# Seven products of halves for 256 channels of gate and up, from chunk 4 on, with partial sums kept in PSUM

## The chip, the cores and the metric

The kernel runs on one core of one Trainium2 chip, in float32 inputs and outputs. The metric is the time of one execution on the device, in microseconds; the kernel before takes 1945.81 us, the median of 3 runs (1944.42 to 1949.61). The engines: PE multiplies matrices (PEld is its loading of weights), DVE, ACT and POOL work element by element, and SP here issues the DMAs. Each engine takes its instructions strictly in the order in which the program wrote them.

## The reference

One block of a network over x of 8192 rows (tokens) and 448 channels, in two halves:

```python
mod = (_silu(c) @ w_mod).reshape(c.shape[0], 6, 1, -1)
sa, ca, ga, sb, cb, gb = (mod[:, 0], mod[:, 1], mod[:, 2], mod[:, 3], mod[:, 4], mod[:, 5])
h = _layernorm(x) * (1 + ca) + sa
x = x + ga * spectral(h)           # rfft, two complex block layers, shrinkage, irfft
h = _layernorm(x) * (1 + cb) + sb
x = x + gb * ((_gelu(h @ w_gate) * (h @ w_up)) @ w_down)    # 448 -> 1792 -> 448
```

The change touches the last two lines.

## The kernel before

Up to 390 us of the profile the spectral part runs; its last inverse transform is done later, chunk by chunk. What follows is the feed-forward part: 32 chunks (`nch`) of 256 rows, each as two blocks b of 128. Float32 accuracy comes from splitting: every operand is a high and a low f16 part, and a product is three matmuls (high x high, high x low, low x high).

**Gate and up** (`gate_up`, L1124). Each chunk has 14 blocks k of 128 features; k = 2t and 2t + 1 are a pair t with q = 0, 1. The feature block is the weight side (128x128), the rows are the moving side (256 columns), and gate and up (pr = 0, 1) lie in one PSUM bank. The 448 channels are three tiles of 128 and a fourth, composed tile that holds the last 64 channels' high and low parts. So a block takes 20 full matmuls in the order of `seq` (L1132), and one half-row matmul for each pr, over 64 channels, which two pairs share in a batch of eight (L1140), two at a time on the upper and lower half of the array. Then `gate_up_out` (L1148): gelu on ACT (L1151), gate times up on DVE (L1156) into x8 tiles and, once both q are there, four additions and subtractions on POOL (the "sums", L1162 to L1165), which prepare the down product. `quantize` (L1167) makes the f16 pair: ACT the high part (L1173), DVE the low part (L1174). It is called one pair later.

**Down** (`down`, L1186) has already seven products of halves in place of eight: 147 matmuls of 224 columns (L1181 to L1183), after k = 2 of the following chunk. Its order on PE is p1 and the 1,1 product (b1, b2), then p4, u2, u4, p7, p3. Product banks rotate over two of tag "pd" (and one of "pc" for b2), so that the product for u2 needs the bank that ACT's copy of p1 (L1208) frees. POOL finishes the output (L1220, L1195, L1196) and SP stores it (L1228).

**Preparing a chunk.** `hooks` (L1233) say behind which block k of a chunk each step for a later chunk stands: loads at k = 0; splitting of v and g (ACT, and POOL at L124) at 3; `inverse` (six f32 matmuls on PE) at 6; `residual` at 7; statistics, square root and normalisation at 8 to 12 (DVE); at 13 `pack_hi` (ACT) and `pack_lo` (POOL, L1077 to L1079). `transposes_dma` (L1081) turns 16 tiles of 128x128 by DMA on SP's queue, one chunk ahead, at k = 0. All of it is under manual schedule: the order of the program is the order on each engine, and nothing is reordered. In the profiled execution chunk 2 begins at 478.35 us, and its down product, that of chunk 1, at 485.55.

## Time and profile before

| | |
|---|---|
| median of 3 runs | 1945.81 us |
| profiled execution: time, span | 1943.83 us, 1942.0 us |
| mean granted clock of PE | 0.993 |
| time of chunk 2 (478.35 to 526.35 us) | 48.00 us |
| DVE, ACT, POOL busy in it | 25.24, 15.46, 31.14 us |

How to read the lines below: a line of the timeline is start, length, engine, source line and operation, what is written and read, how many instructions, and in brackets the idle time ahead of it with what ended it. In a group, the two numbers behind the bar are busy time in all and the mean length of one instruction in nanoseconds. [...] "issue" means that nothing in the profile shows a wait.

### The profile page before, as it was taken

What the parts mean: (1) busy time and instruction counts of PE and PEld (TensorE: products, weight loads), DVE (VectorE), ACT (ScalarE), POOL (GpSimd) and SP (SyncE); (2) the same over time, 40 slices, a digit from 0 to 9 for tenths busy, and PEclk for the clock granted to TensorE, in tenths of its full rate; (3) what the DMA queues carried; (4) which work ended last, traced back from release to release, by engine and by line L of the source; (5) the groups of instructions that cost most, each with busy time, mean ns of one, the idle gap of its engine ahead of it and who ended that gap; (6) DMA issues with size and microseconds to landing.
All of it is one profiled execution on the core that took longest, in us unless ns stands there. A gap on an engine that the chain in (4) does not pass through costs nothing.

```text
span 1942.0 us, 43274 instructions
## 1 busy us (share of the span) xinstructions
PE 1899.8 (98%) x17606; PEld 1690.5 (87%) x17606; DVE 1130.9 (58%) x2340; ACT 779.2 (40%) x1325; POOL 1209.8 (62%) x1492
## 2 busy tenths in 40 slices
PE   7799999899999999999999999999999999999998
PEld 3599999688888888888888888888888888888898
DVE  7687889677555555555555555555555555555533
ACT  5677788553333333333333333333333333333322
POOL 3366689355666666666666666666666666666644
PEclk9899999899999999999999999999999999999999
DMA  9888768431111111111111111111111111111000
GB/s 388 289 275 253 223 192 246 136 97 54 43 44 44 44 43 43 44 43 43 44 44 43 44 43 44 44 43 43 44 43 44 43 44 44 43 43 44 21 16 20
DMA packets 144398, 164.39 MB, mean 85 GB/s; under 512 B 85062, under 2 KB 117062, under 8 KB 143814
## 3 DMA queue, kind: packets, MB, share of 16 engines
q1 hardware_dynamic: 144198, 161.62, 27.6%
q8 instruction: 138, 2.26, 0.5%
q14 instruction: 62, 0.51, 0.1%
HBM read 98.29 MB, written 47.25 MB: 75 GB/s over the span
## 4 chain that ended last, share of the span: by engine, by line
PE 78%; DVE 1%; POOL 1%; DMA 1%; ACT 0%; issue 0%; SPq 0%; POOLq 0%; ACTq 0%
PE pgu L1115 53%; PE pdn L1183 8%; PE pdn L1182 8%; PE pdn L1181 8%; PE pi L1015 1%; PE pi L1013 1%; PE pi L1014 1%; DMA dr<-wdd 0%; DVE ac L1174 0%; DVE n L1065 0%; POOL x L1163 0%; DVE n L1064 0%; DMA vd<-us 0%; POOL x L1162 0%; DMA v<-vd 0%
## 5 line engine op out<-in xcount | busy, mean ns | idle before, releaser
L1115 PE MATMUL pgu<-nt,wh 128*128 128x256 f16 x6272 | 832.8, 273 | 0.2 <-DVE nt L1106 0.2
L1115 PEld LDWEIGHTS <-wh 128*128 128x128 f16 x6272 | 602.0, 98 | 97.3 <-issue 30.3
L1151 ACT ACTIVATE gel<-pgu,dg 128x256 f32<-128x256 f32 x448 | 200.0, 473 | 779.8 <-PE pgu L1115 744.8
L1115 PE MATMUL pgu<-nt,wl 128*128 128x256 f16 (+1 forms) x3584 | 500.9, 272 | 0.7 <-DVE x L1156 0.7
L1183 PE MATMUL pdn<-wd,ac 128*128 128x224 f16 x1568 | 406.1, 259 | 1.1 <-DVE ac L1174 1.1
L1181 PE MATMUL pdn<-wd,ac 128*128 128x224 f16 x1568 | 406.1, 259 | 0.0
L1182 PE MATMUL pdn<-wd,ac 128*128 128x224 f16 x1568 | 406.1, 259 | 0.0
L1162 POOL TENSOR_TENSOR x<-x 128x128 f32<-128x128 f32 x223 | 240.5, 1078 | 241.1 <-DVE x L1156 233.3
L1174 DVE SCALAR_TENSOR_TENSOR ac<-x,sa_act,ac 128x896 f16<-128x896 f32 (+1 forms) x225 | 308.3, 1370 | 86.5 <-ACT ac L1173 86.5
L1115 PEld LDWEIGHTS <-wl 128*128 128x128 f16 (+1 forms) x3584 | 297.6, 97 | 57.6 <-issue 24.6
L1156 DVE TENSOR_TENSOR x<-pgu,gel 128x256 f32<-128x256 f32 x448 | 179.0, 417 | 271.4 <-ACT gel L1151 270.7
L1173 ACT ACTIVATE ac<-x,sa_act 128x896 f16<-128x896 f32 (+1 forms) x225 | 233.0, 1035 | 57.3 <-POOL x L1165 55.2
L1220 POOL TENSOR_TENSOR o<-u,p 128x224 f32<-128x224 f32 x32 | 21.4, 667 | 300.8 <-DVE u L1219 300.8
L1163 POOL TENSOR_TENSOR x<-x 128x128 f32<-128x128 f32 x223 | 159.3, 714 | 17.5
L1183 PEld LDWEIGHTS <-ac 128*128 128x128 f16 x1568 | 153.4, 98 | 1.6 <-DVE ac L1174 1.6
L1181 PEld LDWEIGHTS <-ac 128*128 128x128 f16 x1568 | 153.4, 98 | 0.8 <-ACT ac L1173 0.3
L1182 PEld LDWEIGHTS <-ac 128*128 128x128 f16 x1568 | 153.4, 98 | 0.4
L1164 POOL TENSOR_TENSOR x<-x 128x128 f32<-128x128 f32 x223 | 113.4, 509 | 0.0
L1165 POOL TENSOR_TENSOR x<-x 128x128 f32<-128x128 f32 x223 | 110.5, 496 | 0.0
L561 POOL TENSOR_TENSOR yl<-y,yh 128x448 fp32r<-128x448 f32 x63 | 75.5, 1213 | 40.3 <-ACT yh L556 36.4
L1195 POOL TENSOR_TENSOR o<-o,gb_r 128x448 f32<-128x448 f32 (+1 forms) x64 | 71.9, 1123 | 11.2 <-DVE o L1209 5.6
L1214 DVE TENSOR_TENSOR u<-pdn,p 128x224 f32<-128x224 f32 x32 | 12.5, 392 | 110.9 <-PE pdn L1183 110.9
(268 smaller groups left out, 2870.3 us busy)
## 6 DMA issues: line engine op xcount, KB each, us to landing
raw<-in_gu SPq DMA_DIRECT2D x28, 512.0 KB, 5.4
vd<-us SPq DMA_DIRECT2D x64, 224.0 KB, 3.3
xx<-in_x SPq DMA_DIRECT2D x32, 448.0 KB, 3.2
v<-vd SPq DMA_DIRECT2D x64, 224.0 KB, 2.8
out<-x SPq DMA_DIRECT2D x31, 448.0 KB, 2.7
tr<-td SPq DMA_DIRECT2D x22, 448.0 KB, 6.9
nt<-pk SPq DMA_TRANSPOSE x488, 2.3
tb<-in_x SPq DMA_DIRECT2D x8, 896.0 KB, 17.9
```

The source lines that it names most:

```text
L1115: T.matmul(pgu[i, t, q][:, pr * H : (pr + 1) * H], w[rows, tw, f0 : f0 + 128], nts[i][rows, tn, :], start=start, stop=stop, skip_group_che ...
L1151: S.activation(gl, ps[:, :H], AF.Gelu_apprx_tanh, scale=dg)
L1156: V.tensor_tensor(dst, ps[:, H : 2 * H].rearrange("p (b c) -> p b c", b=2), gl.rearrange("p (b c) -> p b c", b=2), ALU.mult)
L1162: e.tensor_tensor(s1, a21, a22, ALU.add)
L1163: e.tensor_tensor(s2, s1, a11, ALU.subtract)
L1164: e.tensor_tensor(s3, a11, a21, ALU.subtract)
L1165: e.tensor_tensor(s4, a12, s2, ALU.subtract)
L1173: S.activation(ac[:, 0, k], x[:, k], AF.Copy, scale=sc)
L1174: V.scalar_tensor_tensor(ac[:, 1, k], x[:, k], sc, ac[:, 0, k], op0=ALU.mult, op1=ALU.subtract)
L1181: T.matmul(ps, ac[:, 0, ka], wds[t][:, 0, kb], start=t == 0, stop=False)
L1182: T.matmul(ps, ac[:, 0, ka], wds[t][:, 1, kb], start=False, stop=False)
L1183: T.matmul(ps, ac[:, 1, ka], wds[t][:, 0, kb], start=False, stop=t == NP - 1)
```

## The change

From chunk 4 on (`C0`), gate and up of the first two channel tiles are done as one 2x2 product of halves: channels 0 to 127 and 128 to 255 on the one side, row blocks b, feature blocks q = 0, 1. Seven products of 128 columns (Winograd's form) stand for eight. Each is again three matmuls for gate and three for up. The third and fourth channel tile stay as they were (`rest`, `rest_half`), with 256 columns.

The partial sums of the seven products stay in PSUM: a pair has two banks, E and D, from two rings of three. ACT copies one quarter of E to D, another to SBUF (`c5`) and one inside E, DVE adds twice with a result in PSUM, and PE goes on accumulating on what they wrote. A pair passes through three periods: `front1` and `front2`, then `mid`, then `back_e` and `back_d` with gelu, product and sums. quant_hi comes one period later, quant_lo two. One period works on three pairs.

```diff
+        def front1(a):
...
+            prod(a, e, 1, a_of(t, 0, 0), 0, True)
+            prod(a, e, 0, a_of(t, 1, 0), 4)
+            d = ds[a] = ring("D", n)
+            S.copy(quarter(d, 0), quarter(e, 1))
...
+            S.copy(c5, quarter(e, 0))
+        def front2(a):
+            prod(a, es[a], 1, s_of(a[1], 0), 5)
+            V.tensor_tensor(quarter(ds[a], 1), quarter(es[a], 1), c5s[a], ALU.add)
+        def mid(b):
+            e = es[b]
+            prod(b, e, 1, s_of(b[1], 2), 6)
+            S.copy(quarter(e, 0), quarter(e, 1))
+            V.tensor_tensor(quarter(e, 1), quarter(e, 1), c5s.pop(b), ALU.add)
+        def back_e(c):
+            e = es[c]
+            prod(c, e, 0, a_of(c[1], 1, 1), 7)
+            rest(c, 1, e)
+            rest_half(c)
+            out_gelu(*c, 1, e)
+        def back_d(c):
+            d = ds[c]
+            prod(c, d, 0, a_of(c[1], 0, 1), 2)
+            prod(c, d, 1, s_of(c[1], 1), 3)
+            rest(c, 0, d)
+            out_gelu(*c, 0, d)
+            out_mult(*c, 0, d)
+            out_sums(*c)
+        def period(n, hook):
+            a, b, c = (pair(n - j) for j in range(3))
+            if a:
+                front1(a)
+            if n == C0 * NP:
+                quantize(C0 - 1, NP - 1)
+            if pair(n - 4) and (n - 4) % NP != NP - 1:
+                quant_lo(*pair(n - 4))
+            if b:
+                mid(b)
+            hook(0)
+            if c:
+                back_e(c)
+            if a:
+                front2(a)
+            if c:
+                out_mult(*c, 1, es.pop(c))
+            if pair(n - 3):
+                quant_hi(*pair(n - 3))
+            if c:
+                back_d(c)
+                del ds[c]
+            hook(1)
```

The sums of weights (three for each t and pr) are made in chunk 2, one block behind each k; in chunk 3 one more sum overwrites a weight that is no longer needed as it was. Both load their raw weights again by DMA on SP's queue, into two buffers:

```diff
+        def make_s(t, pr):
+            r = raws_s.pop((t, pr)).rearrange("p i k c -> p (i k) c")
...
+            G.tensor_tensor(r[:, 3], r[:, 2], r[:, 3], ALU.add)
+            G.tensor_tensor(r[:, 2], r[:, 0], r[:, 2], ALU.subtract)
+            G.tensor_tensor(r[:, 0], r[:, 3], r[:, 0], ALU.subtract)
+            G.tensor_tensor(r[:, 1], r[:, 1], r[:, 0], ALU.subtract)
+            w_split(shs[t][:, 0, pr], shs[t][:, 1, pr], r[:, 0:3], pr)
+        for i in range(C0):
...
             for k in range(NFT):
                 gate_up(i, k)
...
                 if k == 2 and i > 0:
                     down(i - 1)
...
+                run_hooks(hooks, i, k)
+                t, pr = divmod(k, 2)
+                if i == C0 - 2:
+                    if k > 0:
+                        make_s(*divmod(k - 1, 2))
+                    load_s(t, pr, 0)
+                if i == C0 - 1:
+                    if k == 0:
+                        make_s(NP - 1, 1)
+                    elif k > 1:
+                        make_s1(*divmod(k - 2, 2))
+                    if k > 0:
+                        load_s(*divmod(k - 1, 2), 1)
```

`w_split` is one operation on ACT and one on DVE. The preparation of a chunk moves. From chunk 4 on `hooks2` holds, keyed by 2t + 0 (`hook(0)`) or 1:

```diff
+        hooks2 = {
+            2: [(2, split_g), (2, split_v)],
+            4: [(1, transposes_dma, 0, 16), (2, inverse, slice(0, D), "pd"), (2, residual)],
+            12: [(2, pack_hi)],
+            13: [(2, pack_lo)],
+        }
+        amid = {
+            "b1": [(stats2,), (rsqrt_part, 5)],
+            "b2": [(rsqrt_part, 9), (norm2, 0)],
+            "u2": [(norm2, 1)],
+            "u4": [(combos,)],
+        }
```

`amid` puts statistics and normalisation between the DVE steps of down, which now stands behind t = 2 of the next chunk, and whose b2 is also a "pd" bank. `combos` is four new subtractions of 128 columns on DVE, which make the sums of rows and channels. `pack_hi` and `pack_lo` take 1280 columns (768 in the subtraction before), and a chunk has 22 DMA transposes: 16 at t = 2, the other six behind down and its store. One normalised buffer now holds the low part of v too, and the scales of the rows and weights are made smaller by a power of two. At the end, behind the last period, quant_lo of the third-last pair, quant_hi and quant_lo of the second-last one and both of the last stand ahead of the last down.

## The prediction

> **What bounds the kernel now.** I read the page first: busy time by engine, and the chain that ended last.

> ```profile
> PE 1899.8 (98%) x17606; PEld 1690.5 (87%) x17606; DVE 1130.9 (58%) x2340; ACT 779.2 (40%) x1325; POOL 1209.8 (62%) x1492
> PE pgu L1115 53%; PE pdn L1183 8%; PE pdn L1182 8%; PE pdn L1181 8%; PE pi L1015 1%; PE pi L1013 1%; PE pi L1014 1%; DMA dr<-wdd 0%; DVE ac L1174 0%; DVE n L1065 0%; POOL x L1163 0%; DVE n L1064 0%; DMA vd<-us 0%; POOL x L1162 0%; DMA v<-vd 0%
> L1115 PE MATMUL pgu<-nt,wh 128*128 128x256 f16 x6272 | 832.8, 273 | 0.2 <-DVE nt L1106 0.2
> L1115 PEld LDWEIGHTS <-wh 128*128 128x128 f16 x6272 | 602.0, 98 | 97.3 <-issue 30.3
> ...
> L1156 DVE TENSOR_TENSOR x<-pgu,gel 128x256 f32<-128x256 f32 x448 | 179.0, 417 | 271.4 <-ACT gel L1151 270.7
> ```

> TensorE, nothing else: gate and up (L1115) are half of the chain and wait 0.2 us in all. So work taken from PE is time saved, as long as no other engine gets in PE's way. The windows of chunk 2 and of a later chunk give the others' load, and the timeline gives the cadence:

> ```profile
> core 0: us, PE busy (x) PEld busy (x) DVE busy (x) ACT busy (x) POOL busy (x), PEclk, DMA share, GB/s
> 478.35:526.35 48.00, 48.00 (x459) 42.97 (x456) 25.24 (x51) 15.46 (x25) 31.14 (x41) 1.00 0.22 64
> ...
> 1001.01 0.93 PE L1115 MATMUL pgu<-nt,wh 128*128 128x256 f16 x7
> 1002.10 0.93 PE L1115 MATMUL pgu<-nt,wh 128*128 128x256 f16 x7
> ```

> Seven plus three matmuls start in 1.09 us: 109 ns for 256 columns. POOL works 31 of 48 us; it is the fullest engine after PE, and its queue is in order.

> **PE: what the change saves.** Per pair of feature blocks, before: 40 matmuls of 256 columns (4.36 us) and half of a batch of eight half-row matmuls. After: 7 products x 2 (gate, up) x 3 = 42 matmuls of 128 columns, each with a weight load of its own, 16 of 256, and four half-row ones. The prices of the narrow and the half-row ones:

> ```profile
> 205.38 0.22 PE L410 MATMUL ps<-s,th 128*112 128x128 f16 x1
> ...
> 205.99 0.22 PE L412 MATMUL ps<-s,tl 128*112 128x128 f16 x1
> ```
> ```profile
> 1008.32 1.03 PE L1115 MATMUL pgu<-nt,wl 128*128 128x256 f16 x11
> 1009.29 0.94 PE L1115 MATMUL pgu<-nt,wh 128*128 128x256 f16 x7
> 1009.28 0.66 PEld L1115 LDWEIGHTS <-wh 128*128 128x128 f16 x7 [0.21 <-issue]
> ```

> The spectral stage already runs 128-column f16 matmuls that each load new weights: twelve starts from 205.38 to 205.99, 55.5 ns each. The batch of eight halves costs 1009.29 - 1008.32 less three full ones, 0.64 us, so 0.32 a pair. They go two at a time (0.109 us per two), and the remaining 0.20 us is the pause around the batch, which the change pays for every pair: 0.22 + 0.20 = 0.42. After: 42 x 0.0555 + 16 x 0.109 + 0.42 = 2.33 + 1.74 + 0.42 = 4.50 us; before: 4.68. **Saved: 0.185 us a pair, 36 us over 28 x 7 pairs.** The pause eats a third of what seven products instead of eight give.

> [...]

> **The build of the sums' weights (chunks 2 and 3).** Each k of chunk 2 loads two raw blocks, makes sums on POOL (four 128x128 operations), rounds on ACT and subtracts on DVE. The load sits on SP behind the 16 transposes of the next chunk, and POOL and ACT wait for it in order:

> ```profile
> 482.43 21.27 SPq L1085 DMA_TRANSPOSE nt<-pk  x16
> 510.37 0.46 SPq L917 DMA_DIRECT2D g<-cgm  x1
> g<-cgm SPq DMA_DIRECT2D x32, 128.0 KB, 2.9
> 478.35 0.82 PE L1115 MATMUL pgu<-nt,wh 128*128 128x256 f16 x6
> 485.55 0.26 PE L1181 MATMUL pdn<-wd,ac 128*128 128x224 f16 x1
> 489.49 0.35 ACT L1208 COPY p<-pdn 128x224 f32<-128x224 f32 x1 [3.26 <-PE pdn L1183]
> 491.79 0.35 ACT L1213 COPY p<-pdn 128x224 f32<-128x224 f32 x1 [1.95 <-PE pdn L1183]
> 1925.08 0.62 ACT L1173 ACTIVATE ac<-x,sa_act 128x384 f16<-128x384 f32 x1 [1.19 <-DVE x L1156]
> ```

> SP is free of the transposes at 503.7; the first load is two DMAs of 128 KB, each like that of g (0.46 us to issue, 2.9 to land), and is there at about 507.3. POOL's four sums (each 0.42 us, rows below) end at 509.0, ACT's 384-wide rounding at 509.6. The copy of p1 (L1208) stands behind it on ACT, and behind one gelu: 510.4 instead of 489.5. PE has the next product's bank only then; it was ready at 491.7. **Stall: 18.6 us.** Between the two copies PE ran 24 matmuls in 2.30 us, 96 ns each; down's 147 take 14.1. From 510.4 PE needs 84 of them (8.0 us), eleven blocks (24.0), three batches of halves (1.9) and about 1 for an inverse: to 545. POOL has, from 507.3 on, 13 blocks' four sums (21.5 us) and most of the chunk's own 31.1 us (some 25: five pairs' sums, the output's, the split, the residual): to 554, and between them it waits for ACT and DVE. PE is **10 us late** (0 to 18).

> In chunk 3 the transposes are 22 (29.2 us at that row's 1.33 each), starting 4.1 us into the chunk (482.43 - 478.35). The one-block load behind them lands at 36.6 us, ACT is held from the end of down until 37.3, and gelu and product free the banks at 38.4. PE wants them after three blocks (20 matmuls of 0.109 each, 6.5 us), 14.1 of down, three more blocks and a batch of halves (7.2): 27.8. **Stall: 10.6 us.** Together 39 us (20 to 55; below 0 is excluded, nothing is removed here).

> **The new steady state, 28 chunks.** Work that comes onto other engines in a 4.50 us period: ACT three copies of 128x256, DVE two additions whose result goes to PSUM. No row writes PSUM from ACT or DVE; the nearest are the 0.35 us copy above and DVE's L1156 at 0.42. I take 0.37 and 0.42. With two gelus and one quant_hi ACT then works 3.1 of 4.50 us, and DVE with two products and one quant_lo 2.8; at twice the price 4.2 and 3.7. PE's next use is a good microsecond away, so these cost nothing by themselves. What does cost is order:

> ```profile
> 1001.81 0.72 DVE L1156 TENSOR_TENSOR x<-pgu,gel 128x256 f32<-128x256 f32 x2
> 1002.45 1.14 DVE L1174 SCALAR_TENSOR_TENSOR ac<-x,sa_act,ac 128x896 f16<-128x896 f32 x1
> 1002.62 1.29 POOL L1162 TENSOR_TENSOR x<-x 128x128 f32<-128x128 f32 x1 [1.60 <-DVE x L1156]
> 1003.99 0.46 POOL L1163 TENSOR_TENSOR x<-x 128x128 f32<-128x128 f32 x1
> 1004.41 0.45 POOL L1164 TENSOR_TENSOR x<-x 128x128 f32<-128x128 f32 x1
> 1004.83 0.45 POOL L1165 TENSOR_TENSOR x<-x 128x128 f32<-128x128 f32 x1
> 1005.31 1.04 ACT L1173 ACTIVATE ac<-x,sa_act 128x896 f16<-128x896 f32 x1 [0.35 <-POOL x L1165]
> 1002.30 0.47 ACT L1151 ACTIVATE gel<-pgu,dg 128x256 f32<-128x256 f32 x1 [0.63 <-PE pgu L1115]
> ```
> ```profile
> 1014.66 0.43 POOL L1077 TENSOR_TENSOR pk<-n,pk 128x128 f16<-128x128 f32 x1
> 1015.03 0.30 POOL L1078 COPY pk<-pk 128x128 f16<-128x128 f16 x1
> 1015.28 1.65 POOL L1079 TENSOR_TENSOR pk<-n,pk 128x768 f16<-128x768 f32 x1
> 1015.81 2.06 DVE L1174 SCALAR_TENSOR_TENSOR ac<-x,sa_act,ac 128x896 f16<-128x896 f32 x1 [1.01 <-ACT ac L1173]
> 1016.88 1.31 POOL L1162 TENSOR_TENSOR x<-x 128x128 f32<-128x128 f32 x1
> 1036.81 0.73 POOL L124 TENSOR_TENSOR gl<-g,gh 128x256 fp32r<-128x256 f32 x1
> 1037.49 2.10 POOL L124 TENSOR_TENSOR vl<-v,vh 128x896 fp32r<-128x896 f32 x1
> ```

> The four sums take 2.75 us from the end of DVE's product (1002.53 to 5.28), since the first one runs against DVE's quant_lo (1.29 instead of 0.46); alone they take 1.65. Now follow one period: gelu 0.47, product 0.42, sums 2.75, quant_hi 1.04, two hand-overs of 0.03 (1005.28 to 1005.31), then the next gelu behind it on ACT: a loop of 4.74 us against PE's 4.50. It slips 0.24 us a period from t = 3 on, some 0.8 us by the next chunk's t = 0; down, with its 14 us of PE work, resets it.

> Then POOL's queue over the chunk border. The diff puts the split of g and v in t = 1 and the inverse that needs it in t = 2, one period apart; before, three blocks lay between. Ahead of the split on POOL are, from t = 0: sums (2.75, from the product's end at 1.1 us: 0.2 for PE's last result, gelu, product; 1.9 with the slip), pack_lo with 1280 instead of 768 columns (0.37 + 2 x 0.27 + 2.75 = 3.6), quant_lo's turn in it (0.83, as 1015.81 and 1016.88 show: one waits for the other), the next sums (1.65), then gl and vl (2.8). That is 11.6 us: vl is there at 12.7 to 13.5 us. PE wants it in the third matmul of the inverse: two periods (9.0), 18 narrow matmuls (1.0) and two of 448 columns (0.4) into the chunk, at 10.4. **Stall: 2.3 to 3.1 us, I take 2.7, in 26 chunks (inverse for chunks 6 to 31): 70 us.** With no clash at all it would be 0.4 (10 us).

> Other edits: statistics and normalisation moved into down run on DVE there with some 0.5 us to spare before PE wants a bank (0, at most 14 us in all). 22 transposes end some 3 us before they are used: 0; what is late next is pack_hi, on ACT. Filling the pipeline: 2 us; the end, where quant of the last pairs comes behind the last matmuls: 2 us.

> **Sum,** on the profiled execution: 1943.8 - 36 + 39 + 70 + 4 = 2021. It lies 2 us under the median of the runs, 1945.8, so I say 2022.

> **Rivals.** (1) *PE alone counts:* loads come early and POOL keeps up, as its 62% suggests. 1945.8 - 36 + 0 to 15 = 1910 to 1925. Against it: the queues are in order, and each of the waits follows from their order. 0.12. (2) *Only the build is paid:* POOL and DVE clash less than in the rows and the split is there in time: 1945.8 - 36 + 39 + 4 + up to 13 = 1953 to 1966. 0.15. (3) *Weight loads bound the narrow matmuls,* so that seven products are dearer than eight: it decides from 62 ns a matmul on (24 wide ones, 2.616 us, over 42). For it: a load's own row is 98 ns (PEld, L1115), and a narrow matmul gives it only 54 ns of streaming to hide under. At the full 98 ns PE takes 42 x 0.0425 = 1.78 us more in each of 196 pairs, 350 us, but POOL is then in time: 1945.8 - 36 + 39 + 4 + 350 = 2303, and less in proportion to what is hidden. Against it: the 55.5 ns. 0.03. [...] (4) *DVE is late in down as well,* 0.5 to 1 us in each of 28 chunks, on top of the forecast and its larger stalls: 2055 to 2090. 0.05. My forecast, build and POOL's queue together, 1975 to 2055: 0.65.

> **Numbers.** A measurement here tells 0.3% (6 us) from no change. Faster: rival 1 (0.12) and a part of rival 2 (0.03), where half of the build is hidden too; same 0.05, from rival 2 again; slower 0.80. The range of 1950 to 2055 leaves out rivals 1, 3 and 4, which hold 0.20.

> **What would show it.** Narrow products 55 to 56 ns apart; a pair at 4.50 us where PE does not wait; in chunk 2's down a hole of 18 us ahead of its fourth product, ended by ACT's copy of p1; in chunk 3 one of 10 us; once a chunk a hole of 2 to 3 us in the inverse, ended by POOL's vl. I am wrong if PE stays at 98% (rival 1), if the holes lie elsewhere, or if the products stand further apart than 62 ns.

## The result, and the profile after

The kernel after takes 2108.13 us (median of 4 runs, 2105.63 to 2112.41), the kernel before 1945.12 in the runs beside it: a ratio of 1.084 (1.081 to 1.086). The change makes the kernel slower by 163 us, where 77 were forecast. The profiled execution has a span of 2105.9 us. Its page, busy times, granted clock, the start of the chain and the groups that are new:

```profile
PE 1940.9 (92%) x21137; PEld 1706.1 (81%) x21137; DVE 1298.7 (62%) x2877; ACT 981.3 (47%) x1942; POOL 1252.8 (59%) x1591
PEclk9899999898888999999999999999999999999999
PE 36%; POOL 28%; ACT 7%; DVE 5%; issue 3%; SPq 2%; DMA 1%; POOLq 0%; ACTq 0%
L1280 PE MATMUL ring<-nt,wh 128*128 128x128 f16 x3136 | 332.8, 222 | 11.2 <-DVE x L1224 11.2
L1325 ACT COPY ring<-ring 128x256 f32<-128x256 f32 x196 | 70.0, 357 | 325.1 <-PE ring L1280 249.8
L1331 DVE TENSOR_TENSOR ring<-ring,rc 128x256 f32<-128x256 f32 x196 | 84.4, 430 | 125.2 <-PE ring L1280 125.0
```

PE is no longer on the chain for nearly all of the span: POOL, ACT and DVE have 40% of it. The copies and additions inside PSUM cost 357 and 430 ns, against the 0.37 and 0.42 us of the forecast. And the row PEclk, by fortieths of the span, is 8 four times in a row where the weights' sums are built (474 to 684 us); its two other dips are in the kernel before as well. The mean granted clock is 0.957, before 0.993. Next, from the timeline of PE in a later chunk, the groups at which a period starts and the inverse:

```profile
996.60 0.39 PE L1309 MATMUL ring<-nt,wl 64*128 64x256 f16 x4
...
1001.12 0.39 PE L1309 MATMUL ring<-nt,wl 64*128 64x256 f16 x4
1001.45 0.51 PE L1280 MATMUL ring<-nt,sh 128*128 128x128 f16 x6
1001.79 0.28 PE L1280 MATMUL ring<-nt,wh 128*128 128x128 f16 x2
...
1017.48 0.27 PE L1280 MATMUL ring<-nt,wh 128*128 128x128 f16 x2 [0.42 <-DVE x L1224]
1018.46 0.45 PE L1036 MATMUL pi<-vo,gh 128*128 128x448 f32 x1
1018.86 0.47 PE L1037 MATMUL pi<-vo,gl 128*128 128x448 f32 x1
1020.90 0.47 PE L1038 MATMUL pi<-vn,gh 128*128 128x448 f32 x1 [1.58 <-POOL vn L125]
...
1022.21 0.85 PE L1294 MATMUL ring<-nt,wh 128*128 128x256 f16 x3
...
1026.03 0.49 PE L1294 MATMUL ring<-nt,wh 128*128 128x256 f16 x3
```

Where nothing waits, a period is 1001.12 - 996.60 = 4.52 us (forecast 4.50), and six narrow products take 1001.79 - 1001.45 = 0.34 us, 57 ns each (from start to start; the row of a single one is 222 ns long, as L1280 above shows). So PE's own saving is there. The hole in the inverse is there too, ended by POOL's vl (the tile is named vn here). What no row of the forecast has is the line at 1022.21: three matmuls of 256 columns take 0.85 us, and 4 us later 0.49. The same stretch in windows of 3.41 us:

```profile
core 0: us, PE busy (x) PEld busy (x) DVE busy (x) ACT busy (x) POOL busy (x), PEclk, DMA share, GB/s
1015.26:1018.67 3.41, 2.99 (x44) 2.69 (x41) 2.17 (x4) 1.76 (x4) 3.33 (x6) 1.00 0.06 14
1018.67:1022.09 3.42, 1.84 (x11) 1.14 (x11) 2.51 (x4) 1.81 (x5) 3.42 (x3) 1.00 0.11 22
1022.09:1025.50 3.41, 3.41 (x26) 2.23 (x24) 1.14 (x4) 0.79 (x2) 3.33 (x6) 0.50 0.15 31
1025.50:1028.91 3.41, 3.41 (x41) 3.32 (x39) 2.01 (x4) 1.09 (x2) 0.95 (x2) 1.00 0.14 29
```

The start of the down product in each chunk, read from the trace, tells where the 163.9 us between the two spans (2105.9 and 1942.0) arise:

| stretch | before | after | difference | forecast |
|---|---|---|---|---|
| to down in chunk 2 | 485.5 | 485.0 | -0.5 | 0 |
| from there to down in chunk 4 (build and filling) | 96.5 | 187.7 | +91.2 | 39, and 2 for filling |
| from there 25 chunks on | 1205.6 | 1275.4 | +69.8 | 25 x (2.7 - 1.3) = 35 |
| from there to the last down | 135.2 | 131.7 | -3.5 | -3.9 |
| the last down | 14.4 | 21.3 | +6.9 | 2 |

The last row ends with the last matmul; what follows it takes some 4.8 us in both kernels. Of the 25 chunks in the third row, 21 hold one window at half clock and take 51.2 us; four hold none and take 49.7. Before, they took 48.0 and 48.5 in turn.

### The profile page after: what moved, and what is told of

The parts are those of the page before. It is cut to its first block, busy times and chain, and to the rows that moved or that the text cites. A ratio compares the mean times of both kernels' runs of the same rounds, so it can differ in the third digit from the quotient of the medians.

```text
span 2105.9 us, 51710 instructions
## 1 busy us (share of the span) xinstructions
PE 1940.9 (92%) x21137; PEld 1706.1 (81%) x21137; DVE 1298.7 (62%) x2877; ACT 981.3 (47%) x1942; POOL 1252.8 (59%) x1591
## 3 DMA queue, kind: packets, MB, share of 16 engines
q1 hardware_dynamic: 182502, 172.65, 27.8%
## 4 chain that ended last, share of the span: by engine, by line
PE 36%; POOL 28%; ACT 7%; DVE 5%; issue 3%; SPq 2%; DMA 1%; POOLq 0%; ACTq 0%
POOL x L1232 9%; PE pdn L1414 7%; PE pdn L1416 7%; PE pdn L1415 7%; PE ring L1280 6%; PE ring L1294 6%; ACT ac L1240 4%; POOL x L1233 4%; POOL pk L1126 3%; POOL x L1235 3%; DVE x L1224 3%; POOL vn L125 3%; ACT gel L1215 2%; SPq L1146 2%; POOL x L1234 2%
## 5 line engine op out<-in xcount | busy, mean ns | idle before, releaser
L1232 POOL TENSOR_TENSOR x<-x 128x128 f32<-128x128 f32 x223 | 275.9, 1237 | 328.5 <-DVE x L1224 320.2
L1414 PE MATMUL pdn<-wd,ac 128*128 128x224 f16 x1568 | 409.2, 261 | 23.9 <-ACT p L1445 18.1
L1294 PE MATMUL ring<-nt,wh 128*128 128x256 f16 x2352 | 379.4, 280 | 0.0
L1224 DVE TENSOR_TENSOR x<-ring,gel 128x256 f32<-128x256 f32 x392 | 164.6, 420 | 308.7 <-ACT gel L1215 308.7
L1280 PE MATMUL ring<-nt,wh 128*128 128x128 f16 x3136 | 332.8, 222 | 11.2 <-DVE x L1224 11.2
L1280 PE MATMUL ring<-nt,sh 128*128 128x128 f16 x3528 | 298.6, 221 | 13.8 <-ACT rc L1327 13.6
L1280 PE MATMUL ring<-nt,wl 128*128 128x128 f16 x1568 | 298.7, 222 | 0.0
L1215 ACT ACTIVATE gel<-ring,dg 128x256 f32<-128x256 f32 x392 | 183.7, 469 | 197.9 <-PE ring L1309 163.3
L1280 PEld LDWEIGHTS <-wh 128*128 128x128 f16 x3136 | 251.9, 99 | 27.2 <-issue 23.7
L1280 PEld LDWEIGHTS <-sh 128*128 128x128 f16 x3528 | 217.3, 99 | 63.7 <-issue 63.7
L1294 PEld LDWEIGHTS <-wh 128*128 128x128 f16 x2352 | 220.3, 101 | 22.0
L1294 PE MATMUL ring<-nt,wl 128*128 128x256 f16 x784 | 219.3, 280 | 0.0
```

Source lines behind the costliest of these rows:

```text
L1215: S.activation(gl, ps[:, :H], AF.Gelu_apprx_tanh, scale=dg)
L1224: V.tensor_tensor(dst, ps[:, H : 2 * H].rearrange("p (b c) -> p b c", b=2), gl.rearrange("p (b c) -> p b c", b=2), ALU.mult)
L1232: e.tensor_tensor(s1, a21, a22, ALU.add)
L1280: T.matmul(o, w(l, pr), nt[:, v * 128 : (v + 1) * 128], start=start and pr == 0 and n == 0, stop=n == 2, skip_group_check=True,)
L1294: T.matmul(ps[:, pr * H : (pr + 1) * H], w[:, tw, f0 : f0 + 128], nt[:, UN[tn] * 128 : UN[tn] * 128 + H], start=False, stop=True, skip_gro ...
L1414: T.matmul(ps, ac[:, 0, ka], wds[t][:, 0, kb], start=t == 0, stop=False)
```

## Experiments: does the clock carry the missing part?

Theory A: a hole costs its length, and if PE idles long enough within one window, half of the next. Rival B: a hole costs its length, and the low clock has another cause. (In the expectations for the holes made to measure, "rival B" is another one: no threshold, every hole costs the clock.)

**The hole filled.** Nine matmuls that nobody needs stand in the hole of the inverse:

```diff
+            pss = [bank(tag, "pi2")[:, cs] for b in range(CB)]
...
                 T.matmul(ps, gl[:, b], vh[:, b, cs], start=False, stop=False)
+                for _ in range(9 if b == 0 and i >= C0 + 2 else 0):
+                    T.matmul(pss[1], wh[:, 0, 0:128], wh[:, 0, 0:D], start=True, stop=True, skip_group_check=True)
```

> Nine matmuls of 448 columns (about 1.7 us, their result is overwritten) stand in the inverse's hole of 1.6 us in each of 26 chunks. PE does more work and waits just as long for the residuals. Theory A: the half-clock windows of the steady state go, about 19 chunks x 1.6 us: 2108 - 30 = 2078, with chunks of 49.7 us. Rival B (the half clock has nothing to do with that hole): 2108, or up to 5 us more.

Measured: 2077.22 us, 31 less than after, with more work. One chunk of that kernel as a window (columns as above), and behind it one of the kernel after that has no half clock:

```profile
1021.20:1070.80 49.60, 49.21 (x598) 43.46 (x596) 30.69 (x68) 22.46 (x47) 31.41 (x42) 1.00 0.17 46
```
```profile
924.00:973.70 49.70, 47.70 (x591) 42.70 (x587) 30.68 (x68) 22.46 (x47) 31.53 (x42) 1.00 0.17 47
```

Both chunks are equally long; only the idle time has become busy time, and with it the half clock is gone from all 25 (mean clock 0.974, in after 0.957). Over those chunks the kernel gains 33.6 us. That is the clock's part of the 69.8.

**Holes made to measure, in the kernel before.** In each of 28 chunks one matmul waits for a chain of n copies on ACT behind a gelu; it writes a bank that is overwritten.

```diff
+            z = zs.pop((i, t, q), None)
+            if z is not None:
+                T.matmul(pgu[i, t, q][:, :H], z[:, 0:128], z, start=True, stop=True, skip_group_check=True)
...
+            if 4 <= i < nch and q == 1 and t in (3, 4) and not first_pair:
+                z = zs[(i, t + 1, 0)] = cp.tile([128, H], F16, tag="z", name="z")
+                S.copy(z, gels[(i, t)])
+                for _ in range(2):
+                    S.copy(z, z)
```

One copy:

> The kernel before, with one hole made in PE's work in each of 28 chunks: a matmul (overwritten later) waits for one 128x256 copy on ACT behind the gelu of the block before it. Hole by rows about 0.9 us (gelu 0.47, copy 0.35, hand-overs). Theory A (a window of 3.41 us in which PE idles 1.9 us or more is followed by one at half clock): no half clock, 28 x 0.9 = 25, so 1944 + 25 = 1969. Rival B (no threshold, every hole brings a window at half clock): 28 x (0.9 + 1.7) = 73, 2017.

Three copies:

> As the one with one copy, with three in a row: hole about 1.6 us. Theory A: still under the threshold, 28 x 1.6 = 45, 1989, no window at half clock in the chunks. Rival B: 28 x 3.3 = 92, 2036.

Six copies:

> With six copies: hole about 2.65 us. Theory A: over the threshold where the hole lies mostly in one window, which is so in about half of the chunks or more: 28 x 2.65 = 74 and 14 to 28 windows of 1.7 us, 24 to 48: 2042 to 2066. Rival E (holes cost only their length, the clock follows something else): 2018.

Measured, beside 1943.84: 1979.37 (+35.5, 1.27 a hole), 2005.62 (+61.8, 2.21 a hole) and 2088.38 (+144.5, 5.2 a hole). The mean clock of the first two is 0.993 and 0.992, as in the kernel before, that of the last 0.967. Each chunk of the first two grows by 1.28 and 2.15 us: length alone (the idle time by the profile, about 1.0 and 1.9 us, and the matmul itself). Each hole of six copies idles 3.2 us and, but for one chunk, is followed by a window at half clock, in four chunks by two. All three kernels are slower than theory A's figures, since each hole came out longer than expected; what decides between the theories is the clock. A hole of the middle size, and one of the longest, in the windows of their own grids:

```profile
1116.50:1119.91 3.41, 1.53 (x15) 1.19 (x13) 0.81 (x2) 2.63 (x5) 1.74 (x4) 1.00 0.04 14
1119.91:1123.33 3.42, 3.42 (x35) 2.88 (x35) 2.46 (x4) 0.00 (x0) 2.04 (x2) 1.00 0.00 0
```
```profile
1037.89:1041.31 3.42, 0.33 (x3) 0.31 (x4) 0.42 (x1) 3.23 (x8) 1.73 (x4) 1.00 0.03 10
1041.31:1044.72 3.41, 3.41 (x18) 2.35 (x16) 2.22 (x3) 0.56 (x1) 1.05 (x1) 0.50 0.00 0
```

So the length of a hole counts, and both rivals B fall, the one with another cause and the one for which every hole costs the clock. Of these two windows the one that idles for 1.88 us (3.41 - 1.53) is followed by the full clock, the one that idles for 3.09 us (3.42 - 0.33) by half. Theory A's 1.9 us was the author's estimate; no run shows it as a limit. In the inverse less was enough: 1.58 us, beside f32 matmuls (11 matmuls in that window, 15 in the harmless one). But not always: in the kernel after, 24 windows from 700 to 1900 us idle for 1.56 to 1.58 us, and three of them (from 868.49, 919.69 and 967.48 us) are not followed by half clock.

So PE's idle time alone does not tell these windows apart. Nor does the number of matmuls: the three hold 21, 14 and 20, the other 21 hold 11 to 21. What else decides was not shown.

## Experiments: the steady state

**Inverse half a period later**, from key 4 to key 5 of `hooks2`:

```diff
-            4: [(1, transposes_dma, 0, 16), (2, inverse, slice(0, D), "pd"), (2, residual)],
+            4: [(1, transposes_dma, 0, 16)],
+            5: [(2, inverse, slice(0, D), "pd"), (2, residual)],
```

> Inverse and residual are moved by half a period, from the first to the second hook of t = 2, ahead of down. Theory A: vl is there in time, the hole (1.6 us) and the window at half clock behind it (1.6 us) go in about 24 chunks: 2108 - 70 = 2038 or less, clock about 0.97. Rival C (the wait only moves into down, since the statistics there come behind the residual on POOL): 2095 to 2115, with a hole in down that DVE ends.

Measured: 2111.42 us, rival C. Waits of PE in one chunk:

```profile
PE pdn L1414 <- DVE v L1048: 1.9, 1, 1.9
PE ring L1280 <- ACT rc L1327: 0.6, 1, 0.6
PE ring L1280 <- DVE x L1224: 0.4, 1, 0.4
```

The wait has moved into down. Chunks take 50.7 us; only 4 of the 25 hold a window at half clock (mean clock 0.970, in after 0.957), so most of the clock's part is saved, and spent again on longer waits.

**vl on DVE.** Three places for the same operation: at its old place (ahead of DVE's additions and products of that period), half a period later, and between. For the second and third, vl is taken out of `split` as a subtraction of its own, `split_vl`.

```diff
-                split(n["vh"][:, b, cs], n["vl"][:, b, cs], n["v"][:, b, cs], el=V if i in (0, 1, 3) else G)
+                split(n["vh"][:, b, cs], n["vl"][:, b, cs], n["v"][:, b, cs], el=V if i in (0, 1, 3) or i >= C0 + 2 else G)
```

> The low part of v (vl, 2.09 us on POOL behind pack_lo and two sets of sums) is made on DVE from chunk 6 on. Theory A: the hole in the inverse goes (vl about 1 us ahead of its use) and the half clock with it: chunks of about 47.6 instead of 49.7 and 51.2 us, 26 x 2.0 + 19 x 1.6 = 82 less: 2026. Rival F (DVE is then late for gate times up and the additions in PSUM, as its 2.57 us beside pack_lo suggests): PE's holes stay, with DVE as the one that ends them, 2075 to 2108.

```diff
             2: [(2, split_g), (2, split_v)],
+            3: [(2, split_vl)],
```

> vl is made on DVE as in the run before, but half a period later, behind gate times up and the additions in PSUM; from chunk 6 on. Theory A (order in DVE's queue ended the hole of 1.40 us that was left): that hole shrinks to about 0.4, chunks of 47.5 instead of 48.6, 25 x 1.1 = 27 less than 2056: 2030. Rival F (DVE has too much work there): the hole stays or comes back in the inverse, 2050 to 2060.

```diff
             if c:
                 out_mult(*c, 1, es.pop(c))
+            hook(2)
...
+                    if t == 1 and i + 2 < nch:
+                        split_vl(i + 2)
```

> vl on DVE once more, now between: behind gate times up of q = 1 and ahead of back_d, so neither ahead of the additions in PSUM (hole of 1.40 us) nor behind the last gate times up of the period (hole of 1.7 us in the inverse). Theory A: one hole of 0.4 us is left, no half clock, chunks of 47.5 us: 2056 - 25 x 1.1 = 2029. Rival F (DVE has too much work around quant_lo, 2.57 us beside pack_lo): chunks stay at 48.6 or more, 2056 or above.

Measured: 2056.22, 2112.56 and 2051.97 us. Theory A misses all three; the first and the third lie between A and rival F, the second lies above both. One fence for each kernel, PE's waits from 700 to 1900 us, some 24 chunks (sum, times, longest):

```profile
PE pi L1038 <- POOL vn L125: 37.7, 24, 1.6
PE ring L1280 <- DVE x L1224: 10.3, 25, 0.4
```
```profile
PE ring L1280 <- DVE x L1224: 35.8, 26, 1.4
```
```profile
PE pi L1045 <- DVE vn L1035: 41.6, 24, 1.7
PE ring L1287 <- DVE x L1231: 10.0, 25, 0.7
```
```profile
PE pi L1044 <- POOL gl L125: 19.8, 25, 0.8
PE ring L1287 <- DVE x L1231: 10.4, 25, 0.4
```

They are after, and the three in their order. The first and the third place win 52 and 56 us, although only 0.6 and 0.8 us of waiting a chunk are gone: with 1.4 us, or 1.2 in two pieces, no window falls to half clock (chunks of 48.6 and 48.7 at a clock of 1.00; mean clock 0.972 in both kernels). The second place misses: its hook stands behind the last product of the period, DVE waits there for a gelu, and vl comes 0.15 us later than POOL made it. With this hole of 1.7 us the half clock stays in 21 of the 25 chunks (mean clock 0.956), and the kernel is no faster. The third place was expected at 2029; there the next in the queue, POOL's gl, ends the hole, which the expectation had not seen.

Even so a chunk of 48.7 us is longer than one before (48.2 in the mean). Without any hole it would take 45.8, as the chunk before the last, which has no inverse, and 1.3 for the inverse's six matmuls, most of them 0.2 us apart: 47.1.

## Experiments: the build, the filling, the end

**Without the build** (`load_s`, `make_s`, `make_s1` left out, the sums' tiles set to zero):

> The build of the weights' sums in chunks 2 and 3 is left out (no loads, no sums, no rounding; the seven products run on zeros and on unsummed weights, so the output is not the reference's). Theory A (a hole costs its length and then a window at half clock): down of chunk 3 started 91 us later than it does in the kernel before; without the build 2108 - 91 = 2017, and the mean clock rises from 0.957 to about 0.975. Rival B (holes cost their length alone, the low clock is the load of the new steady state): some 2 x 30 us of holes go, 2048, and the half clock in chunks 2 and 3 stays.

Measured: 2036.74 us (2031 to 2042), between the two. The stretch of the table's second row as one window, in after and then in this kernel, and behind them PE's longest waits in that of after (rc: the raw weights and their sums, but in L1327 the copy `c5`; vo: the high part of v):

```profile
485.00:672.70 187.70, 120.26 (x969) 98.48 (x967) 66.81 (x143) 46.40 (x90) 102.91 (x157) 0.81 0.19 54
```
```profile
490.80:606.50 115.70, 104.08 (x970) 91.26 (x969) 60.78 (x115) 35.13 (x62) 78.80 (x94) 0.94 0.15 41
```
```profile
PE pdn L1414 <- ACT p L1445: 18.1, 1, 18.1
PE pgu L1171 <- DVE x L1224: 13.2, 7, 3.6
PE ring L1280 <- ACT rc L1327: 13.0, 2, 10.2
PE pi L1036 <- ACT vo L123: 6.5, 2, 5.3
PE pdn L1414 <- ACT ac L1240: 5.5, 1, 5.5
```

The build costs 187.7 - 115.7 = 72 us. For the same number of matmuls PE is busy 16.2 us longer, at a clock of 0.81 instead of 0.94, and the remaining 55.8 are waits. Of the two holes that the forecast had, the first is the first row. At the place of the second, in chunk 3 three blocks behind down, ACT does stand for the load behind the transposes (15.65 us, until 612.35), but PE waits only 2.06 us for it (at 613.62). The hole of 10.2 us inside the third row is another one, at 657.72 in chunk 4, as ACT's rows in front of it show:

```profile
656.47 0.40 ACT L1391 ACTIVATE wh<-rc,sw 128x128 f16<-128x128 f32 x1 [5.90 <-POOL rc L1406]
656.78 0.36 ACT L1325 COPY ring<-ring 128x256 f32<-128x256 f32 x1
```

PE waits for the copies of the first new pair; they stand on ACT behind a rounding, which waits for a sum on POOL, and that sum is behind pack_lo (2.60 us from 653.42). And 115.7 - 96.5 = 19 us are there without the build: 15.5 of them where the first new pairs have nothing else beside them, PE waits 3.7 and 3.4 us, and three windows run at half clock.

**The loads on ACT's queue**, so that they don't stand behind the transposes:

```diff
-                dma(r[:, i], wgu[m // 2, pr, :, 0:2, (m % 2) * 128 : (m % 2) * 128 + 128])
+                nc.scalar.dma_start(r[:, i], wgu[m // 2, pr, :, 0:2, (m % 2) * 128 : (m % 2) * 128 + 128])
```

> The raw weights of the build are loaded from ACT's queue, not from SP's behind the transposes. Theory A: the hole of 18.1 us in chunk 2's down and the one of 5.5 us in chunk 3's go with the low clock behind them, 30 to 45 us: 2065 to 2080. Rival D (POOL's four sums for each block are the limit, the loads only the first to be seen): the holes come back at other places, 2095 to 2108.

Measured: 2143.57 us, slower by 35 than after; neither theory had that. ACT's waits in chunks 2 and 3, after first (sh, wh: the rounded sums):

```profile
ACT sh L1391 <- POOL rc L1401: 82.4, 14, 23.0
ACT wh L1391 <- POOL rc L1406: 46.0, 8, 15.7
```
```profile
ACT sh L1391 <- POOL rc L1401: 80.7, 14, 15.7
ACT wh L1391 <- POOL rc L1406: 52.4, 14, 12.3
ACT gel L1215 <- DMA nt<-pk: 19.9, 2, 14.8
```

ACT stands 128 and 133 us for POOL's sums, so the load is only the first thing that it meets. The hole of 18.1 us shrinks to 6.5, and others grow: one of 11.1 in chunk 2, one of 22.8 in chunk 3's down. What the loads on ACT's queue cost beside that, no run shows by itself.

**The rounding one block later.** POOL makes a block's sums at one k, ACT and DVE round them at the next, so that ACT finds them ready. In a second kernel the first two loads stand ahead of the transposes as well, and chunk 3's sums are made at k = 6 to 12, before the pipeline is filled:

```diff
-            w_split(shs[t][:, 0, pr], shs[t][:, 1, pr], r[:, 0:3], pr)
+            return lambda: w_split(shs[t][:, 0, pr], shs[t][:, 1, pr], r[:, 0:3], pr)
...
+                if splits and i >= C0 - 2:
+                    splits.pop()()
...
-                        make_s(*divmod(k - 1, 2))
+                        splits.append(make_s(*divmod(k - 1, 2)))
```

> Build only: the rounding of a block's sums (ACT and DVE) stands one block behind POOL's sums; loads as they were. Theory G (the build's 71 us come from ACT standing in order behind POOL and the loads, 82 and 46 us by its row): PE's holes in chunks 2 and 3 mostly go, with their low clock, 40 to 60 us less: 2050 to 2068. Rival H (POOL has too much work in chunk 2, 31 + 24 us in a chunk of 48): less than 20 us go, 2090 to 2105, and POOL's results end the holes.

> As the one with the late rounding, and the first two loads stand ahead of the transposes; chunk 3's sums follow at k = 6 to 12, gate and up of a t together, and nothing is left for the filling of the pipeline. Theory G: nearly all of the build's 71 us go, 2037 to 2050, and what is left in chunk 3 is the filling (about 11 us of holes). Rival H: chunk 2 stays at 60 us or more for POOL's sake, 2055 to 2080.

Measured: 2087.87 and 2066.73 us, 20 and 41 less than after: the order on ACT and SP is more than half of the build's cost, though less than theory G expected. The first lies just below rival H's range, the second inside it. Is the rest POOL's work? Two of each block's four sums on DVE:

```diff
-            G.tensor_tensor(r[:, 0], r[:, 3], r[:, 0], ALU.subtract)
-            G.tensor_tensor(r[:, 1], r[:, 1], r[:, 0], ALU.subtract)
+            V.tensor_tensor(r[:, 0], r[:, 3], r[:, 0], ALU.subtract)
+            V.tensor_tensor(r[:, 1], r[:, 1], r[:, 0], ALU.subtract)
```

> Late rounding with early loads, 2067, and two of each block's four sums go from POOL to DVE. Rival H (what is left of the build is POOL's work): POOL falls from some 55 to 43 us in chunk 2, and the 20 us by which chunk 2 is still longer than before shrink to 5 or less: 2045 to 2052. Theory G (order alone): 2060 to 2070.

Measured: 2065.34 us. Chunk 2 with all sums on POOL, and with half of them:

```profile
485.10:554.20 69.10, 55.08 (x460) 45.99 (x459) 34.33 (x65) 20.97 (x37) 53.59 (x84) 0.88 0.20 56
```
```profile
486.10:555.90 69.80, 54.98 (x459) 45.96 (x458) 40.50 (x88) 20.69 (x37) 41.52 (x60) 0.88 0.20 56
```

POOL has 12 us less to do, DVE 6 more, and the chunk is as long. So rival H falls as far as it means the amount of POOL's work; its place in the chain of sums and rounding is not tested. Some 30 us remain (2066.73 against 2036.74 without the build). In windows of the table's second row, 146.7 us in that kernel against 115.7, PE is busy for 112.4 and 104.1 us at a clock of 0.86 and 0.94: some 8 us of it are clock and 23 are waits. What makes those waits stays open.

**The filling**, with front1 of the first new pair ahead of the last old block:

```diff
+                if i * NFT + k == C0 * NFT - 1:
+                    front1((C0, 0))
                 gate_up(i, k)
...
-            if a:
+            if a and n > C0 * NP:
                 front1(a)
```

> Late rounding with early loads, and front1 of the first new pair ahead of the last old block, so that PE has work while ACT copies and DVE adds. Theory A (the filling's cost is its holes of 5.1 and 3.4 us and their low clock): 2067 - 8 to 13 = 2054 to 2059. If the holes only move to the next period: 2063 to 2068.

Measured: 2070.77 us, no gain, and over both ranges. The holes of 5.1 and 3.4 us are now one of 7.2, ended by DVE's addition: they only moved.

**Together.** The late rounding with vl half a period later, and then everything with vl in between, without the quant_lo and quant_hi that stood twice at the end:

> Both changes together: late rounding with early loads, and vl on DVE half a period later. If build and steady state add up: 2108 - 65 - 78 = 1965, still over the 1944 of the kernel before, by the filling (about 15 us) and the end (7 us). If PE alone counted it would be 1910.

> All of it: late rounding, early loads, sums on POOL and DVE, vl in between, front1 early, and one quant_lo and one quant_hi fewer at the end, which were done twice. If the parts add up (78 steady state, 41 and 20 build, 10 filling, 3 end): 2108 - 152 = 1956, about 0.6% over the kernel before. Below 1938 would be faster than it.

Measured: 2071.71 us, no better than the build's part alone, as vl stands at the place that misses; and 2013.35 us, 3.5% over the kernel before (ratio 1.0354, 1.0338 to 1.0369). The gains of the parts add up (56 steady state, 41 build: 97, measured 95), but they are smaller than expected. The end gains nothing: the last down takes 21.3 us as in after. No version here beats the kernel before.

## Why the prediction was right or wrong

Direction right, size half. Term by term, in the order of its sum:

- **PE's saving, -36.** Nearly right. A period takes 4.52 us, and 24 narrow products in a row 1.34 (1003.34 to 1004.68 us), 56 ns each. In the kernel before a pair takes 4.69 (the batches of halves at 1052.23 and 1061.61 us stand two pairs apart). So 0.17 us a pair is saved, 1.2 a chunk and 33 in all. Rival 3, weight loads as the bound, is out: it needed more than 62 ns.
- **The build, 39.** The first hole was read rightly, almost to the number: 18.1 us ahead of down's fourth product (18.6). Of the second, place and cause were right, but PE waits 2.06 us there and not 10.6. That another hole of 10.2 us exists is luck: it stands in chunk 4 and hangs on pack_lo and one of POOL's last sums. And the step took the holes for the whole. ACT waits in order for POOL's sums, 128 us in all, and behind it the banks, the inverse or quant. 56 us of waits, and 16 of low clock: 72.
- **POOL's queue over the border, 70.** Right in place and cause, and nearly in size: vl ends the hole in the inverse, chunk after chunk. By the differences the chunks lose 2.6 us to holes (69.8 - 33.6 of clock + 25 x 1.2 of saving, over 25), 66 in all. The rows show 2.4 of them: 1.8 for vl (2.04 between the starts at 1018.86 and 1020.90, 0.2 where nothing waits) and 0.6 ahead of it for DVE's product at 1017.48, which the forecast did not have. PE comes that much later to the inverse, so the two are not independent.
- **Fill 2 and tail 2.** Too small: 19 (of which 3.7 lie in chunk 2, where vl is late without any build) and 7. With nothing beside it, one pair's chain over ACT and DVE lies open, and holes there cost clock as well (three windows without the build).
- **The step that failed** is the one that prices each stall at its length ("Stall: 2.3 to 3.1 us, I take 2.7, in 26 chunks", and likewise for the build). Another 34 us of half clock in the steady state and 16 in the build hang on it, 50 of the 86 that the forecast of 2022 is short of 2108. The next largest miss is the list of the build's stalls, 39 us for 56 of waits. The page before has this row for the clock:

```profile
PEclk9899999899999999999999999999999999999999
```

It stands at 9 almost everywhere, and from 700 to 1900 us no row of the profile has that kernel's PE waiting for another engine; that a clock which never falls says nothing of what a hole would bring, the prediction did not ask.

Sum as measured: -33 (PE) + 72 (build) + 66 (POOL's queue, with DVE's product) + 34 (clock, steady) + 19 (filling) + 7 (end) = 165, against 163.9 between the two spans. The 66 is no measurement of its own: it is what the third row of the table leaves for the holes.

## What to carry to other kernels

In the kernel before no row shows PE waiting for another engine from 700 to 1900 us, and its granted clock is 1.00 there; here the change opened a hole of 1.6 us in each chunk, and paid the hole and, in 21 of 25 chunks, up to half a window (1.7 us) more. The idle time alone did not tell which hole pays: windows with 1.56 to 1.58 us of it were followed by half clock in 21 of 24 cases, one with 1.88 us beside other matmuls was not. Holes of 0.4 and 0.8 us in a chunk left the clock alone where 0.4 and 1.6 did not, and useless matmuls in a hole that can't be closed won 31 us here. Before taking work off the fullest engine, ask what its next operation will wait for: here 1.2 us saved a chunk were more than given back by one subtraction queued behind others on POOL.

## What the runs showed of the hardware that was not expected

**Chunks fell in step with the clock's window.** With half clock a chunk of after takes 51.2 us, which is 15 windows of 3.413 us: the next hole falls at almost the same place of its window. From 1022.09 to 1892.49 us the windows at half clock begin 51.2 us apart, 18 chunks in a row. A chunk of 49.7 us is 14.6 windows, so without half clock the hole moves by half a window from chunk to chunk; after three such chunks the half clock was back.

**DVE and POOL were slower beside each other.** DVE's quant_lo takes 2.57 us beside POOL's pack_lo of 1280 columns; in the prediction's row at 1002.45, beside one of POOL's sums, it took 1.14, and that sum 1.29, where one alone takes 0.46. Timeline of POOL and of DVE in after:

```profile
1012.87 2.62 POOL L1126 TENSOR_TENSOR pk<-vn,pk 128x1280 f16<-128x1280 f32 x1
```
```profile
1013.87 2.57 DVE L1244 SCALAR_TENSOR_TENSOR ac<-x,sa_act,ac 128x896 f16<-128x896 f32 x1
...
1017.02 0.41 DVE L1224 TENSOR_TENSOR x<-ring,gel 128x256 f32<-128x256 f32 x1
```

quant_lo ends 0.95 us after pack_lo does, as if it had waited for it. Two additions and this product queue behind quant_lo, and the product ends PE's wait of 0.42 us at 1017.48. The forecast had seen the pair of rows in the kernel before (2.06 and 1.65), and counted it for POOL only.
